# Attention and routed experts in one launch: operands of 128 rows a head, and the first expert tile inside attention's written order

## The chip, the cores and the metric

The kernel runs on one core of a Trainium2 chip. The metric is the device time of one execution in microseconds. The kernel before took 1025.76 us (median of 3 runs, 1023.96 to 1026.95).

## The reference

Decayed causal attention over 8 batches, 8 heads, 576 positions, head size 64; its output is routed, one expert of eight for each of the 4608 tokens, through a two-layer network.

```python
scores = scale * np.matmul(q, k.transpose(0, 1, 3, 2))
log_f = np.log(np.clip(f, 0.0001, 1.0))
cum = np.cumsum(log_f, axis=-1)
decay = cum[:, :, :, None] - cum[:, :, None, :]
scores = np.where(causal, -1000000000.0, scores + decay)
scores = scores - np.max(scores, axis=-1, keepdims=True)
attn = np.exp(scores)
attn = attn / (np.sum(attn, axis=-1, keepdims=True) + 1e-09)
x = np.matmul(attn, v)                   # then tokens x 512
...
e_idx = np.argmax(x @ w_gate + modality_bias[modality_id], axis=1)
h = np.maximum(x[mask] @ w1[e], 0.0)
out[mask] = gate_w[mask, None] * (h @ w2[e])
```

## The kernel before

**Precision.** Products that must be exact to f32 are made of a high part (a tensor rounded to the matmul's own 32-bit type) and a low part (what the rounding left): high·high + high·low + low·high. The expert layers do this with w1h, w1l, xh, xl, hh, hl, w2h, w2l; the scores do it with X, whose two planes are the high and the low part of k and q.

**Attention** runs over 32 pairs of heads p (four pairs for each batch b). The two heads of a pair lie in rows 0 to 63 and 64 to 127 of a tile, each matmul of 64 rows takes one head, and head 0's and head 1's stand behind each other in the order. For each pair:

- `load_raw` (L323) loads k and q, padded to 1216 columns, on SP's queue; `split_hi` (L327) makes the high part by an ACT cast, `split_lo` (L331) the low part by a subtraction on POOL (on DVE for pair 0). `put_cum` (L337) puts the running sum of log f (as two rows) into Sk by a DMA.
- `max_mm` (L409) makes high-part scores with the running sum to get a bound on each row's maximum: L419 adds the mask, L424 is X·X, L428 the constant columns Cq times Sk, which adds the running sum. `max_red` (L431) reduces them on DVE, `shift_pe` and `shift_split` (L445, L451) turn the maxima into the row mT, and `shift_out` (L458) puts that into Sq with two DMAs.
- `scores` (L468) makes four groups of the transposed scores: L480 the mask, L492 high·high, high·low, low·high and Sk·Sq. `exp` (L494, ACT), `half` and `rest` (L508, L515: P as a high and a low f16 part), `weighted` (L525: L541, L542, L543 are P times v), `divide` (L545: z, then x), the gate (L557 to L590: transposes L568, matmuls L584, `lg` L590), and for each batch `route` (L593), which finds each token's expert and scatters its x to xs in DRAM.

**The order** of all this is written by a planner: every step has its engine, an assumed duration, the steps it follows, and a due time from the table DUE (times PER for each pair). `Plan.order` (L97) then picks, again and again, the step that can start first, with the due time as tie-break, and the instructions are issued in that order: each engine executes its own in that order, whatever is ready.

**The experts** (class `Moe`, L786) come behind attention. 21 full tiles of 256 tokens and at most 8 half tiles run; tables say which rows and which expert each tile has. The first four tiles' table is made early, after batch 5 has been routed (`early`, L1058), the others' by `other_tables` (L908, lines L835 to L891) once tile 0 has been issued. For each tile t `run` (L1064) issues: `load_w1` of t+1, `load_x` of t+2, `split_w2` (L972: casts L976 on ACT, w2l L977 on DVE), `load_w2`, `first(t)` (L994: the first layer, matmuls L1003, hl L1006), `split_w1` (L965: L969 on ACT, w1l L970 on DVE), `prepare(t+1)` (L979: transposes L989, xh L991, xl L992) and `second(t)` (L1008: matmuls L1014, y L1016, a scattering DMA L1017). Here a scheduler of the framework arranges the order on each engine.

Of the kernel before, what the change touches and what calls it, by code (L numbers as in the profile page):

```python
# [24 lines left out]
S = 576  # L25
D = 64
# [34 lines left out]
def f32(ap):  # L61
# [4 lines left out]
PER = 13.5  # L66
DUE = {
# [91 lines left out]
KC, QC = 0, 640  # L159
XW = 1216  # L160


class Attn:
    def __init__(self, ctx, tc, dram, qk, v, f, ids, wg, bias, xs, writers, nb=8):
# [3 lines left out]
        ec = ctx.enter_context  # L168
        pool = lambda name, bufs=1, **kw: ec(tc.tile_pool(name=name, bufs=bufs, **kw))
        self.ps_s = pool("a_s", 3, space=PSUM)  # L170
        self.ps_o = pool("a_o", space=PSUM)
        self.ps_b = pool("a_b", space=PSUM)

        self.vr = pool("a_vr").tile([P, NJ, 512], F32, name="vr")
# [4 lines left out]
        self.qp = pool("a_q", 3)  # L179
# [8 lines left out]
    def setup(self, f, ids, wg, bias):  # L188
# [28 lines left out]
        self.Sk, self.Sq = t([P, 3, QW], F32R, "Sk"), t([P, 3, QW], F32R, "Sq")  # L217
        ones = t([P, P], F32, "ones_f")
        nc.gpsimd.memset(ones, 1.0)
        self.Cq = t([P, P], F32R, "Cq")  # L220
        nc.vector.tensor_scalar(self.Cq, ones, t1, None, ALU.mult)
        nc.gpsimd.memset(f32(self.Sk[:, 0, S:]), 0.0)
        one1 = ones[:, 0:1].rearrange("p (a o) -> p a o", a=1)
        nc.vector.tensor_scalar(self.Sk[:, 0:1, 0:S], one1.broadcast_to([P, 1, S]), t0, None, ALU.mult)
        nc.gpsimd.memset(f32(self.Sk[:, 1:, S:]), 0.0)
# [14 lines left out]
        nc.vector.tensor_scalar(self.Sk[:, 1:3, 0:S], one1.broadcast_to([P, 2, S]), t0, None, ALU.mult)  # L240
        nc.gpsimd.memset(f32(self.Sq[:, 0]), 1.0)
        nc.gpsimd.memset(self.later, 0.0)
        nc.gpsimd.affine_select(self.later, self.later, [[1, P]], ALU.is_ge, -BIG, base=0, channel_multiplier=-1)
        nc.gpsimd.memset(f32(self.Sq[:, 1:]), 1.0)
# [4 lines left out]
        self.Ph_t = [t([P, 2, PW], F16, f"Ph{i}") for i in range(2)]  # L249
        self.Pl_t = [t([P, 2, PW], F16, f"Pl{i}") for i in range(2)]  # L250
        self.lnp = t([P, 1], F32, "lnp")
        nc.vector.memset(self.lnp, math.log(PSC))
        nc.gpsimd.memset(self.vr[64:128, 4, :], 0.0)

# [68 lines left out]
    def load_raw(self, p):  # L323
        raw = self.new(self.rp, "raw", p, [P, XW], F32, 2)
        self.nc.sync.dma_start(raw, self.qk[p])

    def split_hi(self, p):  # L327
        X = self.new(self.qp, "X", p, [P, 2, XW], F32R, 3)
        self.nc.scalar.copy(X[:, 0], self.get("raw", p))

    def split_lo(self, p):  # L331
        X = self.get("X", p)
        self.own(("lo", p % 3), p)
        e = self.nc.gpsimd if p else self.nc.vector
        e.tensor_tensor(X[:, 1], self.get("raw", p), f32(X[:, 0]), ALU.subtract)

    def put_cum(self, p):  # L337

        self.own(("cum", p % 3), p)
        self.nc.sync.dma_start(f32(self.Sk[16:P:32, p % 3, 0:S]), f32(self.chl[2 * p:2 * p + 2]))  # L340
# [68 lines left out]
    def max_mm(self, p, g):  # L409
        nc = self.nc  # L410
        X = self.get("X", p)
        self.owned(("cum", p % 3), p)
# [8 lines left out]
        for c0, w, ic, j0 in segs:  # L421
            for h in range(2):
                r = slice(64 * h, 64 * h + 64)
                nc.tensor.matmul(pm[:, h, c0:c0 + w], X[r, 0, QC - 64 + P * ic:QC + 64 + P * ic], X[r, 0, j0:j0 + w],  # L424
                                 start=not masked, stop=False, skip_group_check=True)
            for h in range(2):
                r = slice(64 * h, 64 * h + 64)
                nc.tensor.matmul(pm[:, h, c0:c0 + w], self.Cq[r], self.Sk[r, p % 3, j0:j0 + w], start=False, stop=True,  # L428
                                 skip_group_check=True)
# [28 lines left out]
    def shift_out(self, p):  # L458
# [3 lines left out]
        for a in range(2):  # L462
            self.nc.sync.dma_start(f32(self.Sq[32 * a:P:64, p % 3, :]), f32(mT[:, a]))
# [297 lines left out]
    def run(self, early=None):  # L761
        self.own("acc", -1)
        with self.tc.manual_schedule():
            self.setup(*self.begin)
            for s in self.steps(early).order():
                s["fn"]()
# [411 lines left out]
```

## Time and profile before

| | |
|---|---|
| median of the runs | 1025.76 us |
| the profiled execution | 1013.86 us (span 1012.1 us) |
| mean granted clock of TensorE | 0.938 |
| attention's pairs | from 25 to 486.6 us, 14.4 us a pair of heads |
| end of the last scores to tile 0's first matmul | 486.6 to 512.5 us |
| 21 full tiles at PE's full pace | 23.4 us a tile |

The profile has one row for each engine's instructions. PE is the matmul array, PEld its weight loads, SPq and POOLq are engines that issue DMAs. A matmul's duration in the timeline overlaps its neighbours', so that the cost of a group is read from its start to the start of what follows it. The granted clock is the share of TensorE's full clock that a throttle let through; the records show 1.0 or 0.5, and a mean between them over a stretch.

### The profile page before, as it was taken

The numbers are of one execution on the slowest core, as the hardware profiler recorded it, in microseconds if no ns is written. First come the engines' busy times: TensorE is split into PE (matmuls) and PEld (weight loads), VectorE is DVE, ScalarE is ACT, GpSimd is POOL, SyncE is SP. The second block draws the span as 40 slices with busy tenths as digits, with TensorE's granted clock in tenths as the row PEclk, the third lists the DMA queues.
The fourth block names the chain that finished last, engine by engine and source line by source line (L and its number), as shares of the span: only waits on it lengthen the run. The fifth ranks groups of instructions, "written<-read, shape, count | busy, mean of one in ns | idle before, by whom it ended". The sixth has DMA issues, their size and how long they took to land. (4 is left out here: it accounts for less than half of the span.)

```text
span 1012.1 us, 22740 instructions
## 1 busy us (share of the span) xinstructions
PE 927.0 (92%) x9347; PEld 808.8 (80%) x9347; DVE 684.1 (68%) x1173; ACT 537.5 (53%) x655; POOL 361.6 (36%) x278
## 2 busy tenths in 40 slices
PE   5999989999999899979689999999999999999792
PEld 3787778777778777768588999999999999999571
DVE  7867978686777858777547766566666666665382
ACT  2765656655756547547443444445444544544371
POOL 7454556865566474653424311111111110111010
PEclk9897999998999969989779999999999999999796
DMA  5212132332321322212302676111111441124640
GB/s 180 77 50 99 33 126 67 99 99 74 97 78 53 99 84 89 87 57 86 131 33 79 218 256 235 43 43 42 53 43 53 134 139 55 43 84 168 234 161 3
DMA packets 38276, 98.22 MB, mean 97 GB/s; under 512 B 3919, under 2 KB 4559, under 8 KB 38160
## 3 DMA queue, kind: packets, MB, share of 16 engines
q1 hardware_dynamic: 31456, 75.60, 22.5%
q0 software_dynamic: 6704, 21.02, 5.5%
q8 instruction: 79, 1.29, 0.6%
q14 instruction: 37, 0.30, 0.1%
HBM read 133.69 MB, written 21.80 MB: 154 GB/s over the span
## 5 line engine op out<-in xcount | busy, mean ns | idle before, releaser
L521 POOL TENSOR_TENSOR Pl<-Pt,Ph 128x1152 f16<-128x1152 f32 (+1 forms) x64 | 152.3, 2385 | 156.2 <-ACT Ph L513 104.4
L502 ACT ACTIVATE Pt<-ps,lnp 128x1024 f32<-128x1024 f32 (+1 forms) x128 | 117.2, 928 | 112.8 <-PE ps L492 104.8
L1017 POOL DMA_INDIRECT out_dram<-y,xg x36 | 47.4, 1316 | 349.4 <-DVE y L1016 333.1
L1003 PE MATMUL ph<-xh,w1h 128*128 128x256 f32 x576 | 164.3, 286 | 2.0 <-ACT xh L991 1.5
L1003 PE MATMUL ph<-xl,w1h 128*128 128x256 f32 x576 | 164.3, 285 | 0.0
L1003 PE MATMUL ph<-xh,w1l 128*128 128x256 f32 x576 | 164.1, 285 | 0.0
L976 ACT CAST w2h<-raw 128x1024 fp32r<-128x1024 f32 x84 | 86.6, 1050 | 115.1 <-PE py L1014 84.7
L970 DVE TENSOR_TENSOR w1l<-raw,w1h 128x1024 fp32r<-128x1024 f32 x80 | 100.9, 1265 | 58.1 <-ACT w1h L969 57.7
L977 DVE TENSOR_TENSOR w2l<-raw,w2h 128x1024 fp32r<-128x1024 f32 x84 | 100.3, 1221 | 56.5 <-ACT w2h L976 55.2
L969 ACT CAST w1h<-raw 128x1024 fp32r<-128x1024 f32 x80 | 83.3, 1048 | 95.6 <-PE ph L1003 57.8
L492 PE MATMUL ps<-X 64*128 64x288 f32 (+4 forms) x1152 | 125.8, 327 | 0.0
L1014 PE MATMUL py<-w2h,hh 128*128 128x512 f32 x312 | 121.6, 398 | 0.0
L1014 PE MATMUL py<-w2l,hh 128*128 128x512 f32 x312 | 119.7, 391 | 0.7 <-DVE w2l L977 0.7
L1014 PE MATMUL py<-w2h,hl 128*128 128x512 f32 x312 | 119.5, 392 | 0.0
L513 ACT CAST Ph<-Pt 128x1024 f16<-128x1024 f32 (+1 forms) x96 | 103.7, 1082 | 21.3 <-PE po L543 20.3
L1003 PEld LDWEIGHTS ph<-xh,w1h 128*128 128x128 f32 x576 | 111.5, 194 | 3.6 <-ACT xh L991 2.4
L1003 PEld LDWEIGHTS ph<-xl,w1h 128*128 128x128 f32 x576 | 111.7, 194 | 0.7
L541 PE MATMUL po<-vh,Ph 128*128 128x65 f16 x960 | 104.9, 202 | 7.5 <-DVE x L554 7.5
L1003 PEld LDWEIGHTS ph<-xh,w1l 128*128 128x128 f32 x576 | 111.7, 194 | 0.0
L543 PE MATMUL po<-vh,Pl 128*128 128x65 f16 x960 | 104.7, 201 | 5.0 <-issue 3.5
L542 PE MATMUL po<-vl,Ph 128*128 128x64 f16 x960 | 104.8, 200 | 1.8 <-issue 1.8
L492 PEld LDWEIGHTS ps<-X 64*128 64x128 f32 x1152 | 93.1, 196 | 13.2 <-issue 1.8
(253 smaller groups left out, 2025.7 us busy)
## 6 DMA issues: line engine op xcount, KB each, us to landing
raw<-in_w_dram SPq DMA_DIRECT2D x84, 1024.0 KB
raw<-in_qk_dram SPq DMA_DIRECT2D x32, 608.0 KB
xg<-xs SPq DMA_DIRECT2D x20, 514.0 KB
vr<-in_v_dram SPq DMA_DIRECT2D x7, 1024.0 KB
raw1b<-in_w_dram SPq DMA_DIRECT2D x4, 1024.0 KB
hxg<-xs SPq DMA_DIRECT2D x5, 257.0 KB
vr<-in_v_dram SPq DMA_DIRECT2D x2, 512.0 KB
vr<-in_v_dram SPq DMA_DIRECT2D x8, 128.0 KB
```

The costliest lines, as they stand in the source:

```text
L492: nc.tensor.matmul(ps[:, h, c0:c0 + w], a, b, start=(j == 0 and not masked), stop=(j == 3), skip_group_check=True)
L502: nc.scalar.activation(self.get("Pt", (p, i))[:, :, o:o + w], ps[:, :, 0:w], AF.Exp, bias=self.lnp, scale=0.125)
L513: self.nc.scalar.copy(self.Ph_t[p % 2][:, :, c], self.get("Pt", (p, i))[:, :, 0:c.stop - c.start])
L521: e.tensor_tensor(self.Pl_t[p % 2][:, :, c], self.get("Pt", (p, i))[:, :, 0:c.stop - c.start], self.Ph_t[p % 2][:, :, c], ALU.subtract)
L541: nc.tensor.matmul(o, Ph[:, c0:c0 + P], vh[:, c, hh, :], start=(c == 0), stop=False)
L542: nc.tensor.matmul(o[:, 1:65], Ph[:, c0:c0 + P], vl[:, c, hh, :], start=False, stop=False)
L543: nc.tensor.matmul(o, Pl[:, c0:c0 + P], vh[:, c, hh, :], start=False, stop=(c == ic))
L970: nc.vector.tensor_tensor(self.w1l[a], self.raw1[i][a], f32(self.w1h[a]), ALU.subtract)
L976: nc.scalar.copy(self.w2h[a], self.raw2[a])
L977: nc.vector.tensor_tensor(self.w2l[a], self.raw2[a], f32(self.w2h[a]), ALU.subtract)
L1003: nc.tensor.matmul(ph[:, i, :], w[:, k, f0:f0 + P], x[:, k, :], start=(j == 0), stop=(j == len(m) - 1))
L1014: nc.tensor.matmul(py, h[:, k, c * P:c * P + P], w[:, k, :], start=(j == 0), stop=(j == len(m) - 1))
```

## The change

**128-row operands.** X, Sk, Sq and Cq go. There are now H (the high part of both heads, two buffers), L (the low part of both heads, three buffers) and A (three buffers), of 128 × 2 × 1280: A[:, h] has the 64 rows of head h's high part in their old place, and in the other 64 rows helper rows: ones, the running sum, the shift and zeros. A matmul of A with A over 128 rows therefore gives high·high with the running sum and the shift. `max_mm` needs one matmul of 128 rows for each head and segment (12 for a pair of heads, not 24 of 64 rows), `scores` one of 128 rows for each head and segment and two of 64 rows, A·L and L·A (36, not 48). The high part is put into A by a new step `put_hi`: two DMAs within SBUF for each pair of heads, 64 × 1280 f32 each (for pair 0 a copy on ACT and one on DVE). `put_cum` has two DMAs, from pair 3 on two more that write zero rows over the old shift; `shift_out` has four. `setup` fills the helper rows by `blank`, on DVE for the first buffer and on POOL for the two others.

**The first tile in attention's order.** The experts' memory pools are rearranged, so that raw1 is there from the start and the others open when attention no longer needs a part of its own. New planner steps do for tile 0 what `run` did: load of w1 and w2, load of x for tiles 0 and 1, split_w1 in four parts, prepare(0) and (1) in two parts each, first(0) in four. `run` keeps split_w2, first and prepare for the later tiles, and second for all. PER and all numbers of DUE are new.

```diff
-PER = 13.5
+PER = 12.5
-    ('setup2',): 36.45, ('hi',): -18.87, ('lo',): -67.23, ('cum',): -14.17, ('mm', 0): -2.46, ('mm', 1): -11.48,
+    ('setup2',): 49.2, ('hi',): -36.74, ('lo',): -86.14, ('cp',): -36.29, ('cum',): 35.07, ('mm', 0): 3.23,
...
+    def put_hi(self, p):
+        self.owned(("hi", p % 2), p)
+        self.own(("A", p % NX), p)
+        H, A = self.H_t[p % 2], self.A_t[p % NX]
+        for h in range(2):
+            r = slice(64 * h, 64 * h + 64)
+            if p:
+                self.nc.sync.dma_start(f32(A[r, h]), f32(H[r]))
+            else:
+                (self.nc.scalar.copy, self.nc.vector.tensor_copy)[h](A[r, h], f32(H[r]))
 
     def put_cum(self, p):
-        self.nc.sync.dma_start(f32(self.Sk[16:P:32, p % 3, 0:S]), f32(self.chl[2 * p:2 * p + 2]))
+        for h in range(2):
+            o = 64 - 64 * h
+            self.nc.sync.dma_start(f32(A[o + 16:o + 64:32, h, 0:S]), f32(self.chl[2 * p + h:2 * p + h + 1]))
+            if p >= NX:
+                self.nc.sync.dma_start(f32(A[o:o + 64:32, h, QW:]), self.zrow)
...
     def max_mm(self, p, g):
-        for c0, w, ic, j0 in segs:
-            for h in range(2):
-                r = slice(64 * h, 64 * h + 64)
-                nc.tensor.matmul(pm[:, h, c0:c0 + w], X[r, 0, QC - 64 + P * ic:QC + 64 + P * ic], X[r, 0, j0:j0 + w],
-                                 start=not masked, stop=False, skip_group_check=True)
-            for h in range(2):
-                r = slice(64 * h, 64 * h + 64)
-                nc.tensor.matmul(pm[:, h, c0:c0 + w], self.Cq[r], self.Sk[r, p % 3, j0:j0 + w], start=False, stop=True,
-                                 skip_group_check=True)
+        for h in range(2):
+            for c0, w, ic, j0 in segs:
+                nc.tensor.matmul(pm[:, h, c0:c0 + w], A[:, h, QC - 64 + P * ic:QC + 64 + P * ic], A[:, h, j0:j0 + w],
+                                 start=not masked, stop=True, skip_group_check=True)
...
     def scores(self, p, g):
+        for h in range(2):
+            for c0, w, c, i0 in segs:
+                k, q = cols(c, w, i0)
+                nc.tensor.matmul(ps[:, h, c0:c0 + w], A[:, h, k], A[:, h, q], start=not masked, stop=False, skip_group_check=True)
         for c0, w, c, i0 in segs:
-            for j, (x, y) in enumerate(((0, 0), (0, 1), (1, 0), (2, 2))):
+            for x in range(2):
                 for h in range(2):
                     r = slice(64 * h, 64 * h + 64)
-                    if x < 2:
-                        a, b = X[r, x, k], X[r, y, q]
-                    else:
-                        a, b = self.Sk[r, p % 3, k], self.Sq[r, p % 3, 64 + i0:64 + i0 + w]
+                    a, b = (A[r, h, k], L[r, q]) if x == 0 else (L[r, k], A[r, h, q])
...
+            last = [("s", n - 1, g) for g in range(4)] + [("vl", nb - 1, c) for c in range(NJ)]
+            add("mw1", (), "SP", 1.1, lambda: moe.load_w1(moe.row[0]), (), [("early",)], d, lands=2.1e6)
+            add("mopen", (), "SP", 0.0, lambda: (self.soon.close(), moe.open_left()), (), last, d)
...
+            add("mw2", (), "SP", 1.1, lambda: moe.load_w2(), (), [("mw1",), ("mopen",)], d, lands=2.1e6)
+            for q in range(4):
+                add("ms", (q,), [("ACT", 1.05), ("DVE", 1.25)], 0, lambda q: moe.split_w1(0, [q]), (q,), [("mw1",), ("mopen",)], d + q)
...
+                add("mf", (g,), [("PE", 2.9), ("ACT", 0.75), ("DVE", 0.75)], 0, lambda g: moe.first(0, [g]), (g,),
+                    [("mp", 1), ("ms", g)], d + 1 + g, take=("ph", g), free=[("ph", g)])
...
     def run(self, acc):
-        self.load_w1(self.row[0])
-        self.load_w2()
-        self.split_w1()
         self.nc.gpsimd.memset(self.raw1[1], 0.0)
-        self.prepare(0)
...
-                self.first(t)
+                if t:
+                    self.first(t)
                 self.split_w1()
-                if t + 1 < FULL:
+                if 1 < t + 1 < FULL:
                     self.prepare(t + 1)
```

What the change moves, at three places. First PE, in the middle of attention, the score group of 320 and 192 columns. Before (X holds both parts of k and q, Sk and Sq the running sum and the shift; L568 is the gate's transpose that follows):

```order
L492 MATMUL ps<-X 128x320 x6
L492 MATMUL ps<-Sq,Sk 128x320 x2
L492 MATMUL ps<-X 128x192 x6
L492 MATMUL ps<-Sq,Sk 128x192 x2
L568 MATMUL pb<-ident,x 128x128
```

Now (the rows of the second head's 128-row matmuls and of the 64-row ones; the first head's two stand ahead of them; the number behind a name is its buffer's):

```order
L519 MATMUL ps<-A_161 128x320
L519 MATMUL ps<-A_161 128x192
L526 MATMUL ps<-L_158,A_161 128x320 x2
L526 MATMUL ps<-A_161,L_158 128x320 x2
L526 MATMUL ps<-L_158,A_161 128x192 x2
L526 MATMUL ps<-A_161,L_158 128x192 x2
```

Sixteen matmuls of 64 rows have become four of 128 rows and eight of 64.

Second SP's queue in the middle of attention, at one of the places where the values of the next batch are loaded. Before (L325 is load_raw, L346 and L348 the values, L463 shift_out, L340 put_cum):

```order
L325 DMA raw<-in_qk_dram 128x1216
L346 DMA vr<-in_v_dram 128x4x512
L348 DMA vr<-in_v_dram 64x512
L463 DMA Sq<-mT 2x5x128 x2
L340 DMA Sk<-chl 4x1x576
```

Now (L340 is load_raw, L497 shift_out, L382 and L384 the values, L364 put_hi, L374 and L376 put_cum with its zero rows, which both follow once more for the other head):

```order
L340 DMA raw<-in_qk_dram 128x1152
L497 DMA A_160<-mT 1x5x128 x4
L382 DMA vr<-in_v_dram 128x4x512
L384 DMA vr<-in_v_dram 64x512
L364 DMA A_159<-H_155 64x1280 x2
L374 DMA A_159<-chl 2x1x576
L376 DMA A_159<-zrow 2x640
```

Eleven transfers of a pair of heads stand where four stood, the two large copies among them, here behind the values.

Third DVE, where the experts begin. Before (w1l and hl belong to tile 0's first layer and the weights of tile 1, the first w2l row to tile 0's second layer; the tables' rows, with names in c_, begin some ten rows further down):

```order
L1006 SCALAR_TENSOR_TENSOR hl<-ph,hh 128x512
L970 TENSOR_TENSOR w1l<-raw_8935,w1h 128x4x256
L1006 SCALAR_TENSOR_TENSOR hl<-ph,hh 128x512
L977 TENSOR_TENSOR w2l<-raw_8950,w2h 128x1024 x4
L992 TENSOR_TENSOR xl<-px_9153,xh 128x4x128
L992 TENSOR_TENSOR xl<-px_9476,xh 128x4x128
```

Now (the last rows of the tables for the other tiles, and tile 0's w2l in them):

```order
L958 TENSOR_TENSOR c_chc<-c_ec 1x8
L955 CAST c_tabb<-c_eb 1x18
L958 TENSOR_TENSOR c_chb<-c_eb 1x18
L1048 TENSOR_TENSOR w2l<-raw_8244,w2h 128x1024 x4
L961 CAST c_tabb<-c_chb 1x18
L960 TENSOR_TENSOR c_chc<-c_chc,c_okc 1x8
L961 CAST c_tabc<-c_chc 1x8
L1078 SCALAR_TENSOR_TENSOR hl<-ph,hh 128x512
```

Tile 0's w2l stands behind nearly all of the tables, and behind the divides and the route of the last batch, which come before them; its hl and w1l stand some eighty rows ahead, in attention's order.

More of the change, by code (lines that the diff above doesn't have):

```diff
@@ L158 @@
 GRP = [(0, 288), (288, 288), (576, 512), (1088, 512)]
-KC, QC = 0, 640
-XW = 1216
+QC = 704
+XW = 1280
+NX = 3
 class Attn:
@@ L216, in setup @@
         make_identity(nc, self.ident)
-        self.Sk, self.Sq = t([P, 3, QW], F32R, "Sk"), t([P, 3, QW], F32R, "Sq")
-        ones = t([P, P], F32, "ones_f")
+        self.H_t = [self.qp.tile([P, XW], F32R, name=f"H{i}") for i in range(2)]
+        self.L_t = [self.qp.tile([P, XW], F32R, name=f"L{i}") for i in range(NX)]
+        self.A_t = [self.qp.tile([P, 2, XW], F32R, name=f"A{i}") for i in range(NX)]
+        ones = self.ones_f = t([P, 1], F32, "ones_f")
         nc.gpsimd.memset(ones, 1.0)
[L220 to L225, printed above, removed]
+        self.t01 = t0, t1
+        self.zrow = t([2, QW], F32, "zrow")
+        nc.gpsimd.memset(self.zrow, 0.0)
+        self.blank(0, nc.vector)
         self.ident16 = t([P, P], BF16, "ident16")
@@ L764, in run @@
             self.setup(*self.begin)
-            for s in self.steps(early).order():
+            for s in self.steps(early, moe).order():
                 s["fn"]()
@@ L825, in open, with open_banks, open_rest @@
         self.hh = one([P, 8, T], F32R, "hh")
         self.hl = one([P, 8, T], F32R, "hl")
+        self.raw2 = one([P, 8, 512], F32, "raw2")
+        self.xgp = pool("xg", 3)
+    def open_banks(self):
+        one, pool = self.tiles(self.ctx)
+        self.px_p = [pool("px", 1, space=PSUM)]
+        self.ps_h = pool("ph", 3, space=PSUM)
+        self.ps_y = pool("py", 2, space=PSUM)
+        self.px = lambda i: self.px_p[i].tile([P, 512], F32, name=f"px{i}")
+    def open_rest(self):
+        one, pool = self.tiles(self.ctx)
+        self.px_p.append(pool("px1", 1, space=PSUM))
@@ L946, in load_x @@
         r = self.val(self.row[t], 1, 8 * (CAP // T) - 1)
-        xg = self.keep.tile([P, 2, 514], F32, name="xg", bufs=3)
+        xg = self.xgp.tile([P, 2, 514], F32, name="xg")
         self.xg[t] = xg
@@ L992, in prepare, with first @@
             nc.vector.tensor_tensor(xl[:, :, c * P:c * P + P], px, f32(a), ALU.subtract)
-    def first(self, t):
+    def first(self, t, part=range(4)):
         nc = self.nc
         xh, xl = self.xh[t], self.xl[t]
-        for g in range(4):
+        for g in part:
             ph = self.ps_h.tile([P, 2, T], F32, name="ph")
@@ L1126, in fused @@
         moe = Moe(keep, tc, w1, w2, xs, writers, out)
+        experts = top.enter_context(ExitStack())
+        moe.open_first(experts)
         with ExitStack() as ctx:
```

183 lines of the change are left out of this document (105 added, 78 removed), and 22 rows, old and new, of the table DUE.

## Prediction

> **What bounds the kernel now.** I read the busy time by stage first. The row is start:end, length, then busy us (and instructions) of PE, PEld, DVE, ACT and POOL, the granted clock, the DMA share and GB/s.
>
> ```profile
> 0.00:25.00 25.00, 13.15 (x81) 9.43 (x83) 18.38 (x35) 7.07 (x8) 18.28 (x56) 1.00 0.57 181
> 25.00:486.60 461.60, 429.43 (x6154) 361.51 (x6152) 347.32 (x728) 288.25 (x343) 262.80 (x158) 0.93 0.25 80
> 486.60:550.00 63.40, 50.94 (x386) 45.90 (x387) 34.95 (x64) 23.87 (x33) 21.42 (x20) 0.76 0.23 80
> 550.00:916.00 366.00, 366.00 (x2388) 335.93 (x2388) 232.51 (x295) 176.78 (x221) 50.05 (x39) 1.00 0.30 105
> ```
>
> Attention (25 to 486.6, 32 pairs of heads, 14.4 us each) is bound by PE: it idles 461.6 − 429.4 = 32 us, while DVE, the next engine, is busy for 75% of the stretch. The experts from 550 on are PE alone, at full clock, and the change doesn't touch them. Between them lies a hand-over in which PE idles 12.5 of 63.4 us and runs at a mean clock of 0.76. So two things can pay: fewer PE microseconds per pair, and a shorter hand-over.
>
> Inside a pair I read PE's timeline at full clock (start, duration, tile; the start of the next group ends a group). First one group of the row maxima, 192 and 320 columns wide, for two heads; it runs from 290.13 to 290.85, 0.72 us:
>
> ```profile
> 290.13 0.35 PE L424 MATMUL ps<-X 64*128 64x192 f32 x2
> 290.33 0.28 PE L428 MATMUL ps<-Sk,Cq 64*128 64x192 f32 x2
> 290.44 0.33 PE L424 MATMUL ps<-X 64*128 64x320 f32 x2
> 290.61 0.31 PE L428 MATMUL ps<-Sk,Cq 64*128 64x320 f32 x2
> 290.85 0.19 PE L623 MATMUL pb<-roh,tri 128*128 128x40 f16 x1
> ```
>
> Then the groups of the scores, and the max groups that follow:
>
> ```profile
> 291.09 0.67 PE L492 MATMUL ps<-X 64*128 64x288 f32 x6
> 291.59 0.30 PE L492 MATMUL ps<-Sq,Sk 64*128 64x288 f32 x2
> 291.82 0.40 PE L480 MATMUL ps<-later,ident 128*128 128x128 bf16 x4
> 292.14 0.70 PE L492 MATMUL ps<-X 64*128 64x320 f32 x6
> ...
> 293.35 0.33 PE L568 MATMUL pb<-ident,x 128*128 128x128 f32 x1
> 293.51 0.33 PE L480 MATMUL ps<-later,ident 128*128 128x128 bf16 x4
> 293.78 0.87 PE L492 MATMUL ps<-X 64*128 64x448 f32 x6
> ...
> 295.15 1.28 PE L584 MATMUL pb<-wg,xT 128*128 128x8 f32 x10
> 296.29 0.33 PE L419 MATMUL ps<-after,ident 128*128 128x64 bf16 x4
> 296.55 0.30 PE L424 MATMUL ps<-X 64*128 64x64 f32 x2
> ...
> 297.29 0.29 PE L424 MATMUL ps<-X 64*128 64x288 f32 x2
> ...
> 297.65 0.29 PE L419 MATMUL ps<-after,ident 128*128 128x128 bf16 x2
> ```
>
> The score groups take 0.73 us (288 columns; there are two), 1.21 (320 and 192) and 1.37 (448 and 64); the max groups 0.74 (64 and 448) and 0.36 for each of two halves of 288.
>
> A matmul of 128 rows is priced by two rows: the experts' (nine of 512 columns from 700.04 to 702.08, so 0.227 each, 0.443 ns a column) and the gate's ten above (128 rows, 8 columns, 295.15 to 296.29: 0.114 each, a floor for narrow ones).
>
> ```profile
> 700.04 0.39 PE L1014 MATMUL py<-w2l,hh 128*128 128x512 f32 x1
> ...
> 702.08 0.39 PE L1014 MATMUL py<-w2l,hh 128*128 128x512 f32 x1
> ```
>
> **The change part by part.**
>
> *128-row operands on PE.* By these prices 448 columns cost 0.198, 320 cost 0.142, 288 cost 0.128, and 192 or 64 the floor of 0.114. Maxima: 192 and 320 become 2 × (0.114 + 0.142) = 0.51, a gain of 0.21; 64 and 448 become 2 × (0.114 + 0.198) = 0.62, a gain of 0.12; a half of 288 becomes 2 × 0.128 = 0.26, a gain of 0.10 twice. That is 0.53. Scores keep two 64-row pairs per segment, which I price like two 128-row matmuls' time: 288 becomes 4 × 0.128 = 0.51, a gain of 0.22 twice; 320 and 192 become 1.02, a gain of 0.19; 448 and 64 become 1.25, a gain of 0.12. That is 0.75, and the total 1.28 a pair of heads. But what is saved is not streaming (the same columns pass: eight 64-row matmuls of 288 stream in pairs, 4 × 0.128 of the 0.73). It is what a group loses around its streams: at its first pair, whose weights nothing hides, and at the change from X to Sq, Sk. The first loss may stay, some 0.1 in each of seven groups: then 0.58 are left. I take 0.85, between these. For 32 pairs: 27 us at full clock, 29 at the granted 0.93. Of a stretch in which DVE is at 75% and ACT at 62%, and which already has 32 us of waiting, I let four fifths come through: **−23**, ends −10 (0.58, half coming through) and −34 (1.28 at four fifths).
>
> A rule of the Trainium skill (TensorE: Matmul & The Clock Gate, Part 3, the mechanism of row tiling) speaks against the saving: matmuls in different row groups run at the same time, starting some 4 ns apart, and a weight load overlaps a running matmul only if the row groups differ, which two 128-row operands never do. The 288 group agrees with the first half: eight matmuls in 0.73 us. By the rule the sum would lose nearly all of this term; it is the second rival.
>
> *Splitting and copying.* The high part costs ACT the same columns in two pieces (1152 for 1216), the low part POOL likewise. New are, on SP's queue, two copies of 64 × 1280 f32 for each pair of heads after the first (655 KB), and single small transfers where one served both heads. The rows of an issue and of a load with its reader:
>
> ```profile
> 304.24 1.10 SPq L463 DMA_DIRECT2D Sq<-mT  x2
> ...
> 12.37 0.34 SPq L325 DMA_DIRECT2D raw<-in_qk_dram  x1
> ...
> 16.46 1.21 ACT L329 CAST X<-raw 128x1216 fp32r<-128x1216 f32 x1 [7.12 <-DMA raw<-in_qk_dram]
> ```
>
> An issue takes 0.55; eleven a pair of heads are 6.1 of SP's 14.4 us, where four were 2.2. A load of 608 KB is there 4.1 us after its issue, so the copy should be too. Bandwidth: 31 × 655 KB over 461.6 us add 44 GB/s to 80, with the queues at a share of 0.25. What this costs is a delay: the max matmuls of a pair now wait for cast (1.2), two issues (1.1) and landing (4.1), 6.4 us where it was 1.2. PE has other pairs' work, and the copy is issued a pair or more ahead: I cost it at 0, from 0 to +8 (for seven value loads of 1.2 MB that stand in front of a copy, up to 1.1 each). If that cover is gone, it is the third rival.
>
> *Start.* POOL and DVE, 18 of 25 us busy in the first stretch, fill the helper rows of three operands, and the first pair is copied by ACT and DVE after its cast, one cast of 1.2 more on the way: **+1.5**, from −1 to +4.
>
> *Hand-over.* Rows of PE, from the last score to the first tile, and of DVE, from the last x to the second tile's start:
>
> ```profile
> 486.32 0.28 PE L492 MATMUL ps<-Sq,Sk 64*128 64x192 f32 x2
> ...
> 512.53 1.01 PE L1003 MATMUL ph<-xh,w1h 128*128 128x256 f32 x3 [0.46 <-ACT xh L991]
> ...
> 557.85 0.48 PE L1014 MATMUL py<-w2h,hh 128*128 128x512 f32 x1
> ```
>
> ```profile
> 508.43 0.49 DVE L554 TENSOR_TENSOR x<-po,z 128x320 f32<-128x320 f32 x1
> ...
> 515.52 0.20 DVE L590 TENSOR_TENSOR lg<-pb,lg 128x40 f32<-128x40 f32 x1 [2.31 <-PE pb L584]
> ...
> 517.75 0.23 DVE L618 TENSOR_REDUCE rtot<-roh 128x8 f32<-128x40 f16 x1
> ...
> 532.17 4.62 DVE L977 TENSOR_TENSOR w2l<-raw,w2h 128x1024 fp32r<-128x1024 f32 x4
> ```
>
> Call the last score's end E (486.6). Before, first(0) starts at E+26 and the second tile's second half at E+71; by then first(0), second(0) and first(1) are done. The work itself, at full clock: 50.9 × 0.76 up to 550, plus 7.9 to 557.85, is 46.6; so 24.7 are idle time and slow clock. After, first(0) stands right behind the last scores. Two waits remain or arise there. First: DVE's four w1l pieces stand ahead of the xl that first(0) needs (four such pieces take 4.62 in the w2l row), and ACT's four casts before them: I estimate 8 us after E. Second: on DVE w2l of tile 0 now stands behind the last divides, the whole route of the last batch and the tables for the other tiles, as the order shows; before, it stood ahead of the tables. The price of the tables:
>
> ```profile
> L970 DVE TENSOR_TENSOR w1l<-raw,w1h 128x1024 fp32r<-128x1024 f32 x4 | 4.9, 1226 | 0.8 <-ACT w1h L969 0.6 <-issue 0.3
> L1006 DVE SCALAR_TENSOR_TENSOR hl<-ph,hh 128x512 fp32r<-128x512 f32 x4 | 2.7, 670 | 0.0
> ...
> L992 DVE TENSOR_TENSOR xl<-px,xh 128x512 fp32r<-128x512 f32 x1 | 0.7, 669 | 0.0
> ```
>
> ```profile
> 549.08 0.15 DVE L842 TENSOR_SCALAR c_nib<-c_nb 1x8 int32<-1x8 f32 x1
> ...
> 563.45 0.15 DVE L890 CAST c_tabc<-c_chc 1x8 int32<-1x8 f32 x1
> ```
>
> They ran from 549.1 to 563.6, 14.5 us, with 4.9 + 2.7 + 0.7 of other work between them and 0.8 idle: some 5.4 of their own. After the last weighted sum DVE and its suppliers need: from x to lg (7.1 in the rows, at half clock, say 5), the route 2.5, ranks and counts some 2, the tables 5.4, the first w2l 1.2: 16. PE has in that time 17 matmuls of first (1.9), the gate's ten (1.1), transposes and ranks (some 1.8): it waits for about 11 us, queued behind its second(0), so that nothing of first(1) can go. Together 46.6 + 8 + 11 + 2 (slow clock after each gap) = E+68, against 71: **−3**, from −12 to +8; if the scheduler's order let all be filled, −18, the first rival.
>
> **Sum.** −23 + 1.5 + 0 − 3 = −24.5, on the profiled execution's 1013.9 us: 989.4. That execution was 11.9 below the median of the runs shown, 1025.8; the same difference carried over gives **1001**.
>
> **The rivals.**
>
> *1. The hand-over is filled* (chance 0.20): DVE gets to w2l in time, since the tables run in PE's shadow. For it: 24.7 us to win. Against: the fixed order on DVE. 15 more: 986.
>
> *2. Streams bound PE, no saving by rows* (0.13): 64-row pairs already run two at a time, and 128-row loads no longer hide. For: the 0.73 for eight matmuls. Against: the experts' 128-row matmuls come every 0.227, which leaves nothing for a load to add. −6 instead of −23: 1018.
>
> *3. PE waits for the copied operand* (0.08): the copy sits on SP behind other transfers and pair after pair arrives late; each wait of PE also brings a slower clock. Decisive from 24.5 / 32 = 0.77 us a pair; at 1.7 us, +31 − 24.5 makes 1032. For: the path of 6.4 us where 1.2 was. Against: the order issues it a pair ahead, and there are three operand buffers.
>
> **How the numbers follow.** The forecast (both gains about as summed) has 0.59. Range: its own terms reach from 983 (−42: all PE gain, −9 at the hand-over) to 1014 (−12); case 1 lies within, case 2 needs 1020, and I stop there. Two measurements of this kernel are told apart from 0.3% (3 us) on: faster is the forecast, cases 1 and 2, less some 0.05 for small remainders; slower is case 3.
>
> **What would show it.** In the changed profile: a 288 score group from 0.73 to about 0.55 and the 192 and 320 max group from 0.72 to 0.55; attention's period from 14.4 to about 13.7; a gap of some 11 us on PE ahead of second(0), released by DVE's w2l; second(1) at E+68. Wrong would be: unchanged group times (case 2), PE waits released by a DMA on A (case 3), or a hand-over without that gap (case 1).

## The result: slower by 4.7%, and the profile after

The changed kernel takes 1071.53 us (median of 4 runs, 1070.16 to 1076.57), the kernel before on the same chip 1024.86 (4 runs, 1020.63 to 1026.95): a ratio of 1.047, interval 1.0429 to 1.0512. The profiled execution took 1076.57 us (span 1074.9). The two profiled executions are 62.7 us apart and the medians 46.7, since before's (1013.86) was shorter than all of its runs listed here and after's is the longest of its four. Stage differences read from the two traces are therefore too large by a third, taken together; the experiments are judged by medians.

The stages after, in the view that the prediction began with (PE, PEld, DVE, ACT, POOL busy; clock; DMA share; GB/s):

```profile
0.00:25.00 25.00, 8.83 (x37) 6.52 (x37) 12.77 (x28) 7.20 (x10) 23.22 (x48) 0.90 0.43 130
25.00:544.70 519.70, 445.47 (x5483) 383.14 (x5483) 373.48 (x736) 293.30 (x375) 291.33 (x213) 0.84 0.39 111
544.70:611.80 67.10, 52.01 (x400) 46.61 (x399) 40.71 (x112) 26.14 (x36) 27.25 (x32) 0.80 0.29 100
611.80:980.00 368.20, 368.20 (x2357) 333.05 (x2356) 228.12 (x252) 176.63 (x220) 44.96 (x35) 1.00 0.30 101
```

The pairs end at 544.7 rather than 486.6. In them PE idles 519.7 − 445.5 = 74 us where it was 32, and its clock falls from 0.93 to 0.84. Since the records show a clock of 1.0 or 0.5 only, each stage can be split: idle time, time in which PE is busy at half clock (half of it is lost), and the work that is left at full clock. E is the last score's end, "start" goes to the fourth pair's shift, and the 15 tiles go from the start of second(1) to that of second(16):

| us | start | pairs to E | of these idle | at half clock | work | E to second(1) | 15 full tiles | rest |
|---|---|---|---|---|---|---|---|---|
| before | 51.2 | 435.4 | 31.3 | 57.4 | 375.4 | 71.2 | 349.9 | 104.3 |
| after | 69.3 | 475.4 | 60.9 | 104.2 | 362.4 | 67.1 | 354.3 | 108.9 |

So the work in the pairs did fall, by 13.0 us, and the hand-over by 4.1. Against that stand 29.6 more of idle time and 23.4 lost to the slow clock in the pairs, 18.1 at the start, 4.4 in the tiles and 4.6 behind them.

What PE waits for, by groups (total, times, longest), in after:

```profile
PE pb L413 <- DVE a L407: 24.3, 7, 4.3
PE ps L460 <- DMA A<-chl: 11.4, 1, 11.4
PE ph L1120 <- PEq L1163: 10.4, 1, 10.4
...
PE py L1086 <- DVE w2l L1048: 6.9, 1, 6.9
...
PE ps L519 <- DMA A<-mT: 5.8, 1, 5.8
...
PE ps L460 <- DMA A<-H: 1.6, 2, 1.2
```

The first row is new: six waits of 3.3 to 4.3 us, one in each of the batches 2 to 7 whose v is scaled, and one of 0.3 at the start. The last is the copied operand, the prediction's third rival: 1.6 us in all. Of the other transfers into A, the running sum holds PE ahead of the very first matmul, and the shift once, up to 39.5 us, a wait that goes with the fills in run 1; the zero rows hold it for 0.9 in all. L413 is a small matmul that spreads a batch's largest |v| over the rows; it needs the reduction L407. DVE's timeline behind one of these waits:

```profile
309.62 0.20 DVE L634 TENSOR_REDUCE rm<-lg 128x5 f32<-128x40 f32 x1
309.85 2.21 DVE L636 TENSOR_TENSOR rd<-lg,rm 128x40 f32<-128x40 f32 x1
312.09 1.31 DVE L640 TENSOR_SCALAR rc<-rd 128x40 f32<-128x40 f32 x1
313.44 1.35 DVE L641 TENSOR_TENSOR rc<-rc,iota_e 128x40 f32<-128x40 f32 x1
314.82 0.20 DVE L644 TENSOR_REDUCE rei<-rc 128x5 f32<-128x40 f32 x1
...
315.39 2.23 DVE L696 TENSOR_SCALAR rse<-rse 128x5 f32<-128x5 f32 x1
...
318.10 0.14 DVE L407 TENSOR_REDUCE a<-pb 1x1 f32<-1x3 f32 x1
```

L407's input is ready from 312.5 (its matmul L405 starts at 312.37), but it stands behind the route of an earlier batch. The route's small operations take 0.2 us or 1.3 to 2.2, and each long one ends where an instruction of POOL ends (312.00, 313.37 inside the second row, 314.73, 317.60):

```profile
307.53 4.47 POOL L555 TENSOR_TENSOR Pl<-Pt,Ph 128x1152 f16<-128x1152 f32 x2
311.96 2.77 POOL L354 TENSOR_TENSOR L<-raw,H 128x576 fp32r<-128x576 f32 x2
315.23 2.37 POOL L555 TENSOR_TENSOR Pl<-Pt,Ph 128x1152 f16<-128x1152 f32 x1 [0.49 <-ACT Ph L547]
```

DVE holds such an instruction until POOL's running one is done; no row calls it a wait, it shows as a duration. Over all eight routes of this execution 25 operations take longer than 0.45 us, and each of the 25 ends 0.03 to 0.06 us behind the end of a POOL instruction that was running when it began. The reductions among them never stretch. The Trainium skill (SBUF — State Buffer, Who interferes with whom) has this rule: DVE and GpSimd share one port pair as an exclusive lock for a whole instruction, taken on DVE by operations with two SBUF inputs and by tensor_scalar in its 2-port modes, never by a reduction. The rows agree: reductions 0.20, the other forms up to 2.23.

The clock after such a wait, in three stretches around another of the six:

```profile
116.30:120.60 4.30, 0.01 (x1) 0.02 (x1) 4.16 (x9) 0.71 (x2) 3.73 (x3) 0.83 0.62 142
120.60:136.30 15.70, 12.86 (x99) 11.21 (x99) 12.20 (x30) 4.79 (x7) 5.84 (x9) 0.50 0.34 114
136.30:150.00 13.70, 13.70 (x189) 11.48 (x187) 8.71 (x17) 10.06 (x11) 7.66 (x4) 1.00 0.49 137
```

After 4.3 us of idling PE runs 15.7 us at half clock: 99 matmuls in 12.9 busy us, then 189 in 13.7. Half of the 12.9, some 6.4 us, is lost to the clock, more than the wait itself.

### The profile page after: what moved, and what is told of

The parts are those of the page before. It is cut to its first block, busy times and chain, and to the rows that moved or that the text cites. A ratio compares the mean times of both kernels' runs of the same rounds, so it can differ in the third digit from the quotient of the medians.

```text
span 1074.9 us, 21733 instructions
## 1 busy us (share of the span) xinstructions
PE 937.1 (87%) x8579; PEld 820.3 (76%) x8579; DVE 703.4 (65%) x1176; ACT 541.6 (50%) x688; POOL 393.4 (37%) x331
## 5 line engine op out<-in xcount | busy, mean ns | idle before, releaser
L555 POOL TENSOR_TENSOR Pl<-Pt,Ph 128x1024 f16<-128x1024 f32 (+1 forms) x64 | 151.1, 2371 | 120.8 <-ACT Ph L547 113.3
L536 ACT ACTIVATE Pt<-ps,lnp 128x576 f32<-128x576 f32 (+1 forms) x128 | 116.1, 928 | 112.3 <-PE ps L526 109.4
L1041 DVE TENSOR_TENSOR w1l<-raw,w1h 128x1024 fp32r<-128x1024 f32 x80 | 97.2, 1224 | 65.6 <-ACT w1h L1040 65.6
L354 POOL TENSOR_TENSOR L<-raw,H 128x576 fp32r<-128x576 f32 x62 | 100.6, 1644 | 68.5 <-PE ps L526 68.4
L1086 PE MATMUL py<-w2h,hl 128*128 128x512 f32 x312 | 121.7, 399 | 0.0
L575 PE MATMUL po<-vh,Ph 128*128 128x65 f16 x960 | 107.8, 204 | 4.6 <-DVE x L588 2.4
L460 PE MATMUL ps<-A 128*128 128x288 f32 (+4 forms) x384 | 96.3, 370 | 14.3 <-DMA A<-chl 11.4
L576 PE MATMUL po<-vl,Ph 128*128 128x64 f16 x960 | 107.5, 202 | 0.0
```

The costliest lines, as they stand in the source:

```text
L354: e.tensor_tensor(L[:, c], y, f32(H[:, c]), ALU.subtract)
L460: nc.tensor.matmul(pm[:, h, c0:c0 + w], A[:, h, QC - 64 + P * ic:QC + 64 + P * ic], A[:, h, j0:j0 + w], start=not masked, stop=True, skip_ ...
L536: nc.scalar.activation(self.get("Pt", (p, i))[:, :, o:o + w], ps[:, :, 0:w], AF.Exp, bias=self.lnp, scale=0.125)
L555: e.tensor_tensor(self.Pl_t[p % 2][:, :, c], self.get("Pt", (p, i))[:, :, 0:c.stop - c.start], self.Ph_t[p % 2][:, :, c], ALU.subtract)
L575: nc.tensor.matmul(o, Ph[:, c0:c0 + P], vh[:, c, hh, :], start=(c == 0), stop=False)
L576: nc.tensor.matmul(o[:, 1:65], Ph[:, c0:c0 + P], vl[:, c, hh, :], start=False, stop=False)
```

## The experiments

**Theories on the first result.** A: the DVE steps that scale v stand badly in the written order, behind the route. B: POOL's instructions stretch the route on DVE, and whatever is queued there waits. Beside them, for the start: the fills on POOL; for the hand-over: the tables ahead of w2l.

**1. The fills on DVE.** In `setup`:

```diff
-        self.blank(1, nc.gpsimd)
+        self.blank(1, nc.vector)
...
-        self.blank(2, nc.gpsimd)
+        self.blank(2, nc.vector)
```

> The changed kernel, with the helper rows of the second and third operand buffer filled on DVE and not on POOL. Theory (the loss sits at two places of the order, the fills on POOL at the start and the matmul that scales v): POOL is free some 14 us earlier, the memset of vr that DVE waits for 7.9 us for comes before 12 us and not at 26, and the first pairs are 10 to 15 us earlier: 1058 (1054 to 1064). Rival (the loss is spread over all pairs, because the operand copied by DMA is late): the start's delay is taken up by later waits, 1068 to 1074.

Measured: 1062.06, ratio 1.0319 (1.0288 to 1.0349), and the start 59.4 rather than 69.3. In after a pair of fills took POOL 3.6 us, where DVE does three in 1.78, and behind the fills the row maxima of v waited:

```profile
22.27 3.57 POOL L268 TENSOR_SCALAR A<-ones_f,t 64x576 fp32r<-64x576 f32 x2
25.89 0.52 POOL L255 MEMSET vr<- 64x512 f32 x1
```

```profile
4.68 1.78 DVE L268 TENSOR_SCALAR A<-ones_f,t 64x640 fp32r<-64x640 f32 x3
...
26.44 0.69 DVE L390 TENSOR_REDUCE am<-vr 128x1 f32<-128x512 f32 x1 [7.92 <-POOL vr L255]
```

Ten of the start's eighteen are the fills. Of the eight that stay, 4.5 are a wait of PE for the first pair's operand, which DVE copies into A.

**2. Theory A: v's scaling moved out of the route's way**, by a pass over the written order for batches 2 to 7:

```diff
+            v3 = o.pop(at(("v3", b)))
+            o.insert(at(("v1", b)) + 2, v3)
+            v2 = o.pop(at(("v2", b)))
+            o.insert(at(("rt", b - 2, 0)), v2)
```

> The changed kernel, with two steps of the preparation of v (the second transpose and the matmul that spreads the scale) put ahead of the route of the batch two back, for batches 2 to 7; nothing else is moved by hand. Theory: six waits of PE of 2.4 to 4.8 us each and the stretches of 14 to 24 us at half clock behind them go: 6 x (4 + 4 to 8) is 48 to 72, so 1000 to 1025. Rival (the wait is only named there; DVE's queue or the copied operand holds the next matmul as long): the same idle time shows in front of other lines, 1055 to 1073.

Measured: 1089.0, ratio 1.06 (1.0533 to 1.0667), slower than the changed kernel. The wait didn't go, it moved to another instruction behind the same route:

```profile
PE po L575 <- DVE x L588: 27.4, 9, 4.2
PE pb L405 <- DVE a L400: 13.2, 5, 2.6
```

Theory A falls: whatever stands behind the route waits.

**3. The tables later**, behind tile 1 rather than tile 0:

```diff
-OTHERS = 1
+OTHERS = 2
```

> The changed kernel, with the tables for the other tiles made after tile 1 and not after tile 0, so that tile 0's w2l no longer stands behind them on DVE. Theory: PE's wait of 6.9 us ahead of tile 0's second layer and some half clock go: 1062 to 1067. Rival (the tables only delay something else, or PE's wait was hidden by later slack): 1070 to 1073.

Measured: 1064.83, ratio 1.0359 (1.0317 to 1.04), with the hand-over 60.7 rather than 67.1. The prediction's wait for w2l is behind the tables, as it said.

**4. All three.**

> The three edits together. Theory: gains at different places add up, about 1071.5 - 13 - 55 - 6 = 997 (985 to 1015), under the kernel before. Rival: over 1040, since one wait has taken the place of another.

Measured: 1080.65, ratio 1.0515 (1.0482 to 1.0549). The reordering loses what the others gain, and PE waits 7.4 us in the first layer of tile 3 (counted from 0) instead. Run 5, without the reordering, has that wait too (7.5); run 3 alone does not. So edit 3 gains by itself and loses its gain beside edit 1. In run 5 ACT and DVE split w2 ahead of the hl that PE waits for, and that w2 is issued on SP's queue at 631.9 us, 28 us after the issues before it; what holds the queue was not tried.

**5. Edits 1 and 3 as a base for the next three**, on a second chip:

> The changed kernel with two of the edits: the fills on DVE and the tables after tile 1. It is the ground of the next three runs. The gains of the two alone were 0.015 and 0.011 of the time before, at different places, so both theories expect a ratio of 1.047 - 0.026 = 1.021 (1.016 to 1.026); what is left is the pairs of attention, which took 40 us more.

Measured: 1067.2. The kernel before scattered on this chip (1001 to 1024), so these four are compared with one another.

**6. The table DUE of before** for the steps that both kernels have, PER 13.5:

> The ground, with PER and the due times of the kernel before for all steps that it had, and a due time of -18 for the copy. Theory 1 (the new order puts the route of each batch against busy stretches of POOL, the operands themselves are right): another order has other collisions, and the blocked time of the route's operations on DVE falls from 38 us to near 14; ratio 0.99 to 1.01. Theory 2 (the operands are to blame: two fetches more on the path of each pair, and a PE that is fed later): the order hardly matters, ratio 1.015 to 1.04.

Measured: 1067.39, from 1051.63 to 1078.5. Inconclusive: the median didn't move, two of its five runs are some 15 below the base (1051.63 and 1053.29), and its own runs are 27 us apart. The traced one, the slowest (1076.8 of span), has some half of the stretch on the route, and more half clock (137.2 us).

**7. Theory B: POOL waits for the route.** For batches 0 to 6 the low-part and Pl subtractions on POOL that stand beside a route go behind it, with a tiny POOL copy ahead that reads the route's last column:

```diff
+    def after_route(self):
+        self.nc.gpsimd.tensor_copy(self.turn, self.done)
...
+            o[j:j] = [dict(name=("turn", b), fn=self.after_route)] + late
```

> The ground, with POOL's large subtractions near a batch's route put behind it: a one-column copy on POOL that reads the route's last result stands ahead of them, in 7 of 8 batches. Theory 1 (DVE's small operations wait for POOL's running instruction, and PE waits for DVE): the route's five stretched operations fall from 2 us to 0.2, PE's wait for a L407 from 26 us to under 8, half clock behind it goes: 25 to 45 us less than the ground, ratio 0.98 to 0.997. Rival (POOL's own result is late then, or DVE's queue is late for other reasons): within 10 us of the ground, 1.01 to 1.03.

Measured: 1029.26 (1022.64 to 1039.17), 38 us below the base on the same chip. Pairs 437.8 against 472.2; idle time 35.7 against 60.2, half clock 75.4 against 99.1. Nothing was taken from any engine's work. The groups of two of the route's operations over all eight batches (busy us, mean ns), after and with this edit:

```profile
L696 DVE TENSOR_SCALAR rse<-rse 128x5 f32<-128x5 f32 x8 | 13.4, 1675 | 0.3
L640 DVE TENSOR_SCALAR rc<-rd 128x40 f32<-128x40 f32 x8 | 11.0, 1374 | 0.2
```

```profile
L655 DVE TENSOR_SCALAR rc<-rd 128x40 f32<-128x40 f32 x8 | 1.5, 182 | 0.2
L711 DVE TENSOR_SCALAR rse<-rse 128x5 f32<-128x5 f32 x8 | 1.4, 172 | 0.3
```

Some 22 us less on DVE in these two groups, and 38 less for the kernel: theory B holds, and run 8 points the same way by other means.

**8. Theory B another way: half of POOL's low-part subtractions on DVE.**

```diff
-        e = self.nc.gpsimd if p else self.nc.vector
+        e = self.nc.gpsimd if p and p % 4 not in (3, 0) else self.nc.vector
```

> The ground, with the low part's subtraction of every third and fourth of four pairs (those next to the route) on DVE and not on POOL; the order is the same. Theory 1: POOL no longer holds DVE there, DVE has 1.5 us more in half of the pairs; 10 to 30 us less than the ground, ratio 0.99 to 1.01. Rival: DVE has more to do and is the later engine: ratio 1.02 to 1.035.

Measured: 1042.62 (1037.78 to 1050.86), 25 below the base although DVE has more to do. The two rows above come to 1.5 and 1.4 us here too; `rd` still stretches (mean 761 ns).

**9. Edits 1 and 7**, the tables back at their place, on a third chip (before 1026.06 there, 1018.03 to 1032.36):

> The changed kernel with the fills on DVE and POOL's subtractions behind the route; the tables where the change put them. Theory (the loss is the fills and DVE behind POOL; the tables' move only shifted a cost of 10 us from tile 0 to tile 2): 1029 - 6 = 1023 on the chip of the last runs, a ratio to before of 0.995 to 1.01. Rival (the tables' move was a gain there): ratio 1.012 to 1.025.

Measured: 1022.11, ratio 0.9967 (0.9929 to 1.0005). The pairs' row, and the same place of DVE's timeline as above, with POOL's:

```profile
25.00:490.90 465.90, 427.64 (x5484) 368.55 (x5484) 342.21 (x732) 292.32 (x373) 277.83 (x189) 0.93 0.43 121
```

```profile
274.83 0.20 DVE L649 TENSOR_REDUCE rm<-lg 128x5 f32<-128x40 f32 x1
275.06 0.20 DVE L651 TENSOR_TENSOR rd<-lg,rm 128x40 f32<-128x40 f32 x1
275.30 0.18 DVE L655 TENSOR_SCALAR rc<-rd 128x40 f32<-128x40 f32 x1
...
276.83 0.23 DVE L667 TENSOR_REDUCE rtot<-roh 128x8 f32<-128x40 f16 x1
```

```profile
272.74 2.37 POOL L556 TENSOR_TENSOR Pl<-Pt,Ph 128x1152 f16<-128x1152 f32 x1
276.56 0.19 POOL L622 COPY turn<-rse 128x1 f32<-128x1 f32 x1 [1.45 <-DVE rse L711]
```

From rm to rtot the route takes 2.2 us, in after 8.5 (309.62 to 318.2); POOL idles 1.45 for it. The clock is before's again (0.93), and PE idles 465.9 − 427.6 = 38 us instead of 74. The later part of the route, behind the POOL copy, is still stretched (L689, rde from rei and rr, has a mean of 1020 ns), and PE waits there for rr, six times 2.0 us.

**10. Without the early tile:** as 9, with the planner's new expert steps left out and `run` loading and preparing tile 0 behind attention.

> d1_best without the first tile in attention's order: its loads, splits, prepare and first layer come behind attention, as before the change; the memory pools stay as the change has them. If the early tile is worth the hand-over's 4 us (67.1 for 71.2 in the traces): 3 to 8 us more than d1_best. Rival (it costs something in attention's last pairs, or is worth the 18 us of all gaps): up to 4 less, or 12 to 20 more.

Measured: 1040.34, ratio 1.0129 (1.0079 to 1.0179), 18 above 9; the hand-over 83.5 rather than 65.0. Among it PE waits for the first tokens, which are loaded behind attention here:

```profile
PE px L1077 <- DMA xg<-xs: 14.6, 2, 12.8
```

So the 18 us are not the early tile alone: 14.6 are this wait. Before issues the same loads at 441 us, 45 ahead of attention's end; here the tokens' buffers open only behind attention, and the loads are issued at 528. Against before's hand-over of 71.2, without an early tile, those of 67.1 and 65.0 are 4 to 6 shorter; against the 62.5 of run 11, which has none either, they are longer. What the early tile is worth by itself stays open.

**11. The kernel before with edit 7 alone** (low parts whose buffer the next load soon needs stay in their place).

> The kernel before, with the same hand-made order of POOL behind the route (a low part whose buffer the next load needs at once stays where it was). There the route's operations were stretched by 14 us in all and PE waited little for them. Theory (the stall hurts where PE waits on DVE right behind the route): -2 to -10 us, ratio 0.99 to 0.998. Rival (putting POOL back costs as much as it gives): 0.998 to 1.008.

Measured: 1009.22 (1002.03 to 1015.08), ratio 0.9817 (0.9764 to 0.9869): the fastest of all, and below both kernels of this study. Before's route was stretched as well, only less:

```profile
L606 DVE TENSOR_SCALAR rc<-rd 128x40 f32<-128x40 f32 x8 | 7.7, 957 | 0.1
L602 DVE TENSOR_TENSOR rd<-lg,rm 128x40 f32<-128x40 f32 x8 | 6.0, 746 | 0.3
```

Its trace still has 6.4 us in the first of these groups. Summed over all stretched groups of the route (what each operation takes over the shortest of its kind) the stretch falls only from 23 to 17 us, so that the 17 us of gain come from it is not shown. In which stage the gain lies the traces don't settle: against before's profiled execution the start is 3.5 and the hand-over 8.6 shorter, the pairs 9 longer.

**12. As 9, with hh and hl in their old place in SBUF**, beside w2h and w2l (raw2 and the xg pool are opened ahead of them):

```diff
+        self.raw2 = one([P, 8, 512], F32, "raw2")
+        self.xgp = pool("xg", 3)
...
-        self.raw2 = one([P, 8, 512], F32, "raw2")
-        self.xgp = pool("xg", 3)
```

> d1_best with hh and hl next to w2h and w2l in SBUF, as in the kernel before (raw2 and the x buffers opened ahead of them). In the changed kernel a matmul of the second layer comes every 0.235 us and not every 0.229, and a tile takes 23.6 us and not 23.3. If the place of hh against w2h does that: 0.229 again and 5 us less than d1_best. If not: 0.235 and the same time within 2 us.

Measured: 1014.81 (1013.5 to 1016.4), ratio 0.9884 (0.9843 to 0.9925), 7 below 9. The 15 tiles take 350.2 instead of 354.2, as before (349.9). The edit moves raw2 and the xg pool along with hh and hl, so which of them matters is not shown.

**13. As 12, with the fills moved back, the second buffer's behind the first pair's copy and the third's behind its shift**, on the chip of runs 1 to 4:

> d4_layout with the helper rows of the second and third operand buffer filled later: the second's behind the first pair's copy, the third's behind the first pair's shift, each with the transfer of the running sum that needs it. In d4_layout the first pair's second matmul waits 4.5 us for the copy on DVE, which stands behind eight fills of 0.6 us, and the fourth pair's maxima are there at 59 us where the kernel before has them at 51. Theory (the fills are what is left of the start's loss on DVE): 4 to 8 us less than d4_layout, a ratio of 0.980 to 0.985. Rival (the fills delay the second and third pair as much, or the copies by DMA on SP do): within 2 us of d4_layout, 0.986 to 0.991.

Measured: 1014.61 (1014.01 to 1020.3), the time of 12; its ratio of 1.005 (1.001 to 1.009) goes against a before that scattered there (1001 to 1034). In the trace, of an execution 5.7 above its median, the start is 3.6 shorter and the pairs 6.6 longer. The wait for the first copy (4.52) goes, and one for a copied operand by DMA comes, 1.90 and then 0.98 more.

## Why the prediction was wrong, point by point

**The failed step** is in "128-row operands on PE" and "Splitting and copying" together: four fifths of a gain were let through, and nothing was put down for the new order of POOL and DVE beyond the copy's delay. The prediction took DVE's durations as its own ("busy for 75%"), so that an order that lays POOL's long subtractions beside the route cost nothing. By runs 5 and 7 these waits cost 38 us, the largest price of all. Not all of it is the change's: summed as in run 11, the route's stretch is 39 us in after and was 23 before, and edit 7 takes 17 off the kernel before. So the change's own share is an estimated 20 of the 46.7 us (38 less 17); some 10 are the fills (run 1), 7 the place of hh and hl (run 12), and some 6 stay with all of it mended (below). Whether the new numbers of DUE or the new operands lay POOL beside the route stays open (run 6). The trace of before had it in sight (L606 at a mean of 957 ns, where its kind takes 180), and no term or rival used it. The copy that it priced instead, and made a rival of, cost 1.6 us; this rival forecast slower, as it came, but for a cause that did not hold. Its price was mis-summed as well: 1.7 us a pair of heads are 54 us over 32 pairs, which would have made 1056 and not 1032. What the prediction said of the clock ("each wait of PE also brings a slower clock") was right and too small: it allowed 2 us, at the hand-over, and 23 more were lost in the pairs.

**PE's work**: forecast 0.85 us a pair of heads, measured 13.0 / 32 = 0.41. By the medians of the groups at full clock, masks included, the maxima gained 0.74 where 0.53 was forecast (64 and 448 from 1.09 to 0.86, 192 and 320 from 1.04 to 0.87, both halves of 288 from 1.14 to 0.80), and the scores lost 0.26 where 0.75 of gain was put. The score group that was forecast at 0.55 takes 0.91 (309.20 to 310.11):

```profile
309.20 0.51 PE L519 MATMUL ps<-A 128*128 128x288 f32 x2
309.64 0.40 PE L526 MATMUL ps<-L,A 64*128 64x288 f32 x2
309.88 0.29 PE L526 MATMUL ps<-A,L 64*128 64x288 f32 x2
310.11 0.20 PE L575 MATMUL po<-vh,Ph 128*128 128x65 f16 x1
...
311.47 0.51 PE L460 MATMUL ps<-A 128*128 128x288 f32 x2
311.82 0.28 PE L456 MATMUL ps<-after,ident 128*128 128x128 bf16 x2
311.92 0.52 PE L460 MATMUL ps<-A 128*128 128x288 f32 x2
312.37 0.16 PE L405 MATMUL pb<-ident,a 3*1 3x3 f32 x1
```

The two 128-row matmuls last 0.44 to the start of the 64-row ones, 0.18 more than 2 × 0.128. Half of that needs no change of rows: in the first max half two such matmuls take 0.35 between neighbours of 128 rows, 0.09 more than 2 × 0.128. The other half stands where 64-row matmuls follow, and the two 64-row pairs behind it take 0.24 and 0.23, where three pairs took 0.50 before (291.09 to 291.59). So a change between 128 and 64 rows seems to cost some 0.1, and the change put one inside every score group; no run changes that alone. The maxima point the same way. Their halves of 288 are no faster (0.35 and 0.45; before 0.36, from the rows at 297.29, and 0.47), but the mask of 128 rows between them, which no longer follows 64-row matmuls, takes 0.10 rather than the 0.21 of before:

```profile
297.86 0.40 PE L424 MATMUL ps<-X 64*128 64x288 f32 x2
...
298.33 0.20 PE L541 MATMUL po<-vh,Ph 128*128 128x65 f16 x1
```

So the prediction's price by streams failed on both, and its second rival was right for the scores. It rested on a rule of the Trainium skill (TensorE: Matmul & The Clock Gate, Part 3: a weight load hides only behind a matmul of another row group), with which the 0.91 agrees, against 0.73 for eight 64-row matmuls. The experts' rows of the prediction do not agree with it: matmuls of 128 rows, each with a weight load of its own, follow each other there every 0.227 us for 512 columns, with no loss. Why a group of two pays and a long run does not stays open.

**Start**: forecast +1.5, measured +18. The fills were counted as instructions on an engine with room; on POOL they take three times DVE's time, and v waited behind them (run 1: ten of the eighteen).

**Hand-over**: the mechanism was right, the total in part by luck. E is 544.7, first(0) starts at E+8.1 (forecast 8), PE waits 6.9 for w2l ahead of second(0) (forecast 11), the second tile's second half starts at E+67.1 (forecast 68):

```profile
544.41 0.29 PE L526 MATMUL ps<-A,L 64*128 64x288 f32 x2
...
552.77 0.58 PE L1075 MATMUL ph<-xh,w1h 128*128 128x256 f32 x1 [0.68 <-ACT xh L1063]
...
594.67 0.80 PE L1086 MATMUL py<-w2l,hh 128*128 128x512 f32 x1 [6.94 <-DVE w2l L1048]
...
611.75 0.48 PE L1086 MATMUL py<-w2h,hh 128*128 128x512 f32 x1
```

The 67.1 are 44.5 of work, 15.1 of idle time and 7.5 lost to half clock, where 46.6, 19 and 2 were put. The first rival (all filled) is out, and run 3 shows that the tables were in the way.

**The experts untouched**: wrong by 4.4 us in 15 tiles, because the change rearranges the pools (run 12 brings them back with hh, hl, raw2 and xg in their old order).

**What the change is worth with all this mended** is read from runs 12 and 11, which have the same POOL order and ran on one chip: 1014.81 against 1009.22, 5.6 slower. By stages of their traces the pairs are 13.1 shorter (431.2 against 444.3), the start 11.7 longer (59.4, 47.7), the hand-over 2.3, the tiles 0.2, and the rest 4.4. By these stages most of the gain in the pairs is paid for at the start, by operands that must be filled and copied before the first pair can run; that is argued from the stages, since run 13, which shortened the start, gained nothing. Most of the 4.4 behind the tiles is a wait of PE's own sequencer ahead of the half tiles (10.4 us in run 12 as in after, 6.6 in run 11), which no run looked into.

## What to carry to other kernels

Read an engine's durations against the shortest of the same form: a small DVE operation that sometimes takes ten times as long, and ends with an instruction of POOL, is a wait that no view lists, and all that is queued behind it shares it. Moving the waiting step doesn't help; keeping POOL's long instructions out of that short stretch does, even by one tiny POOL copy that reads the stretch's result (in these runs the edit took 2% off the kernel before and 4% off the changed one). And price a wait of PE with the slow clock behind it, which can cost more than the wait.

## What the runs showed of the hardware that was not expected

The half-clock stretch behind a wait of 3.3 to 4.3 us lasted from 14 to 24 us at the six waits of after, while one of 3.14 us in before was followed by 3.4 us only. In run 9 six waits of 2.0 us were followed by 6.8 us each, and one of 3.2 by 27. In before 17 us of half clock (360.6 to 377.6) came with no wait longer than 1.2 us in the 15 us ahead of it. What sets the length stays open (PE had further short waits within the long ones). In all traces of this case the granted clock changes only in steps of 3.41 us.

The same matmul of 128 rows and 512 columns comes at another pace when hh and hl, with raw2 and xg, lie elsewhere in SBUF. From 779.99 to 781.62 seven of them take 0.233 each in after; over whole tiles it is 0.235 against 0.229 before:

```profile
779.99 0.39 PE L1086 MATMUL py<-w2l,hh 128*128 128x512 f32 x1
...
781.62 0.39 PE L1086 MATMUL py<-w2h,hl 128*128 128x512 f32 x1
```

Run 12 brings the old pace back (0.229). Which relation of the addresses matters was not tried.
